# Reordering the head of a fused linear-attention and SwiGLU kernel: three passes over the contraction, a second issuing queue, a shorter warm-up

## The chip, the cores and the metric

The kernel runs on one core of a Trainium2 chip. Its time is the device time of one execution in microseconds (us), the median of several runs. A core has TensorE (matrix products, called PE in the profile), VectorE (DVE), ScalarE (ACT), GpSimd (POOL) and SyncE (SP), which here only issues DMA transfers. The engines run at the same time and wait for each other on semaphores. ScalarE can issue transfers too, from its own queue.

## What is computed

For x of 2048 tokens by 640 the reference mixes two branches by a gate per token, all in bf16:

```python
g = sigmoid((x * gate_w).sum(-1, keepdims=True))
return g * A(x) + (1 - g) * B(x)
# A: q, k, v = x @ wqkv in 32 heads of 20; phi(y) = concat(softmax(y @ w_phi), softmax(-y @ w_phi)) per head
#    kv = phi_k^T v;  z = sum of phi_k;  o = phi_q kv / (phi_q z + 1e-6);  A = o @ wo
# B: (silu(x @ w_gate) * (x @ w_up)) @ w_down, with 1728 hidden columns
```

## The kernel before, in words

**Tiling.** The contraction over the 640 columns of x is cut into five chunks of 128 (index c), the tokens into four blocks of 512 (bt) for branch B and 16 tiles of 128 for branch A. The hidden columns of branch B come in 14 groups of 128 (index k; the last has 64). x is loaded already transposed by DMA into `xT` (chunk, token). The gate weights lie in `wg`, the up weights in `wu`, both (chunk, column).

**Branch B.** For a block and a group, five matmuls of 128x128 by 512 columns give the gate product in one PSUM bank, five more the up product in another. `ffn_tail` takes them on: tanh on ACT, a scalar-tensor-tensor step on DVE (which frees the gate's bank), a copy on ACT (which frees the up's), and a product on POOL into `hT`. `down` multiplies `hT` by `wd`.

**Branch A.** `premult` folds w_phi into the q and k weights; `ktile` and `qtile` make the softmax features (`features`), DVE doing most of that work; the q features and the result `ob` are transposed by DMA on SP (`eT`, `oT`) before TensorE uses them.

**What sets the order.** Nothing is left to a scheduler on the chip. `_build` collects tasks, each with an engine, an assumed cost, what it depends on, a priority, and buffers it takes and gives. `_Plan.run` plays them through on the host, always starting on a free engine the ready task of lowest priority number, and the order it finds is the program's order on each engine. The waits on semaphores that the chip needs are put in from the real data accesses. A `load` has an assumed landing time (`land`), to which `L_SLACK` is added where it is over 13 us; loads of one engine are chained, so they go out in the order written. `E_SLACK` and `O_SLACK` are added to the assumed ends of the eT and oT transposes. `K_AT`, `K_EACH`, `Q_AT`, `Q_EACH`, `PRE_AT` are times in the plan before which a tile's features, or a folding of weights, aren't started. All these numbers change only the order, never what is computed.

**The head.** The first thing TensorE can do is groups 0 to 3 (`HD = 4`) of the first token block: 4 groups x 2 products x 5 chunks = 40 matmuls in all eight PSUM banks. Before it, `warm` runs dummy matmuls on a constant. `load_head` loads pieces of the first 512 gate or up columns, `load_x` pieces of x, and `ffn_head` orders the 40 matmuls by the pieces: gate then up on chunks 0-1, then gate of groups 0-1 on chunks 2-3 and chunk 4, gate of groups 2-3 on chunks 2-4, up on chunks 2-4. All the loads are issued by SP; the first eight are the head's. ACT begins with its table load (for tanh and exp), done for the small task called `table`; later it issues one tiny transfer, the gate column `gw`, held until 11.0 in the plan.

Of the kernel before, what the change touches and what calls it, by code (L numbers as in the profile page):

```python
# [6 lines left out]
P = 128  # L7
S_TOK = 2048
D = 640
H = 32  # L10
DH = 20
F_FFN = 1728
# [224 lines left out]
class _Plan:  # L237
# [98 lines left out]
def _mm(*cols):  # L336
    return sum(c / 2400.0 + 0.003 for c in cols)


def _build(  # L340
# [13 lines left out]
    pe, act, dve, pool, sp = nc.tensor, nc.scalar, nc.vector, nc.gpsimd, nc.sync  # L354
    run = tr.run
# [54 lines left out]
    ps = nc.alloc_psum_tensor("ps", [P, 8 * 512], F32)  # L410
# [11 lines left out]
    def one(b, c0, c1, r0=0, r1=P):  # L422
        return ps[r0:r1, b * 512 + c0:b * 512 + c1]
# [56 lines left out]
    v1ones = places(v1all)[:, :, :, DH]  # L480
    v1pad = v1all.rearrange("p (g x) -> p g x", x=WIN)[:, :, WIN - 1]

    L_SLACK, E_SLACK, O_SLACK = 1.0, 1.4, 1.0
    chain = {}

    def load(eng, dst, src, land, prio, transpose=False, name="load", cost=0.06):

        t = add(eng, cost, lambda: dma(eng, dst, src, transpose=transpose), prio=prio, lat=2.0, name=name)
        t.land = land
        t.slack = L_SLACK if land > 13 else 0.0  # L490
        t.after = chain.get(eng)
        chain[eng] = t
        return t

    def rows(a):
        return a.rearrange("(c p) j -> p c j", p=P)
# [50 lines left out]
    ph_l = load("sp", wph[:, :, :], rows(A_w_phi.rearrange("h e f -> (h e) f")), 16.5, -36.2)  # L547
    load_gu(2, "sp", (17.6, 18.8), -36)
    wkT_l = load_wT(1, 21.6, -34)
    load_gu(3, "sp", (23.2, 24.8), -33)  # L550
    wv_l = load("sp", wvg[:, :, 0:D], rows(A_wqkv[:, 2 * D:3 * D]), 27.3, -32)
    xs[2] = load_x(2, -31, (0, 5, 31.0))
    load_gu(4, "sp", (32.4, 33.9), -30)
    wgl[NPC] = load("sp", wg[:, :, 1664:1728], gsrc[:, :, 1664:1728], 34.2, -29)
    wul[NPC] = load("sp", wg[:, :, 1728:1792], usrc[:, :, 1664:1728], 34.6, -28)
    xs[3] = load_x(3, -27, (0, 5, 37.4))
    wqT_l = load_wT(0, 41.5, -26)
    wd_l = [load("sp", wd[:, 0:13, :], rows(B_w_down[0:13 * P, :]), 48.5, -25),
            load("sp", wd[0:64, 13, :], B_w_down[13 * P:F_FFN, :], 49.0, -24)]
    wo_l = load("sp", wo[:, :, :], rows(A_wo), 51.0, -23)  # L560
    xl = [x_[4] for x_ in xs]


# [36 lines left out]

    ones_row = nc.const_aps.tensor(1.0, (P, 512), BF16)

    def warm(banks, before):
        ctx = {}

        def fn():
            for b in banks:
                last = pe.matmul(one(b, 0, 512), lhsT=ones_row[:, 0:P], rhs=ones_row[:, 0:512], start=True, stop=True, skip_group_check=True)
            return last
        b0, b1 = min(banks), max(banks) + 1  # L610
        t = add("pe", 0.427 * len(banks), lambda: run("pe", fn, reads=[], writes=[ps[:, b0 * 512:b1 * 512]]), prio=-10,
                acq=[("bank", ctx, i) for i in range(b0, b1)], rel=[("bank", ctx, i) for i in range(b0, b1)], name="warm")
# [64 lines left out]
    def ffn_head():  # L677
        tsl = slice(0, 512)
        cs = [{} for _ in range(HD)]
        before = warm_t  # L680
        last = {}

        def group(key, c0, c1, parts):
            nonlocal before
            w = wg if key == "g" else wu

            def fn(ks, cc):
                mms([(one(cs[k][key], 0, 512), w[:, c, P * k:P * k + P], xT[:, c, tsl], c == 0, c == 4) for c in cc for k in ks])
            for ks in parts:
                t = add("pe", _mm(*[512] * (len(ks) * (c1 - c0))), lambda ks=ks: fn(ks, range(c0, c1)),  # L690
                        deps=[xs[0][c1 - 1], hw[key, min(c0, 2), ks[-1]]], prio=-5,
                        acq=[("bank", cs[k], key) for k in ks] if c0 == 0 else (), name="head")
# [408 lines left out]
```

## Time and profile before

| | |
|---|---|
| median of 3 runs | 287.67 us (287.45 to 287.74) |
| span of the profiled execution | 285.6 us |
| TensorE busy | 282.2 us (99%), 2050 matmuls |
| DVE, POOL, ACT busy | 223.9, 171.2, 146.2 us |
| weight loads of TensorE (beside its matmuls) | 151.0 us |
| first real matmul | 5.17 us |
| end of the 40 head matmuls | 13.80 us |
| HBM read, written | 8.30 MB, 2.62 MB |

The span runs from the first to the last instruction; the median is 2.0 us above the span of the profiled execution, for which the profile has no row. Matmuls are pipelined: the profile prints 379 ns for one of 512 columns, but in a stream they start 0.216 us apart. "L442" is a line of the kernel; all real matmuls have that line, all dummy ones L608, all DMA issues L470, all ACT operations L452, since helpers record them. SPq and ACTq are the issuing queues: the time beside them is that of issuing, not of the transfer, and "to landing" counts from the start of the issue.

### The profile page before, as it was taken

What the parts mean: (1) busy time and instruction counts of PE and PEld (TensorE: products, weight loads), DVE (VectorE), ACT (ScalarE), POOL (GpSimd) and SP (SyncE); (2) the same over time, 40 slices, a digit from 0 to 9 for tenths busy, and PEclk for the clock granted to TensorE, in tenths of its full rate; (3) what the DMA queues carried; (4) which work ended last, traced back from release to release, by engine and by line L of the source; (5) the groups of instructions that cost most, each with busy time, mean ns of one, the idle gap of its engine ahead of it and who ended that gap; (6) DMA issues with size and microseconds to landing.
All of it is one profiled execution on the core that took longest, in us unless ns stands there. A gap on an engine that the chain in (4) does not pass through costs nothing.

```text
span 285.6 us, 5119 instructions
## 1 busy us (share of the span) xinstructions
PE 282.2 (99%) x2050; PEld 151.0 (53%) x2050; DVE 223.9 (78%) x318; ACT 146.2 (51%) x222; POOL 171.2 (60%) x164
## 2 busy tenths in 40 slices
PE   8999999999999999999999999999999999999996
PEld 3445555455555555655445555555455565545654
DVE  1324299999999999999999977989999978970312
ACT  2555656775756584344563454456655545564110
POOL 5199407686388748663684577676986666665100
DMA  7999999200000000000217517363435335323211
GB/s 178 258 234 268 225 187 330 88 1 1 2 0 2 0 0 2 2 0 0 45 20 82 127 50 143 75 95 76 93 79 96 67 66 117 60 39 75 69 48 46
DMA packets 65848, 23.91 MB, mean 84 GB/s; under 512 B 53984, under 2 KB 65824, under 8 KB 65824
## 3 DMA queue, kind: packets, MB, share of 16 engines
q1 hardware_dynamic: 65168, 23.58, 38.5%
q8 instruction: 16, 0.26, 0.4%
q10 hardware_dynamic: 656, 0.00, 0.1%
q14 instruction: 8, 0.07, 0.1%
HBM read 8.30 MB, written 2.62 MB: 38 GB/s over the span
## 4 chain that ended last, share of the span: by engine, by line
PE 97%; DMA 1%; SPq 0%; DVE 0%; issue 0%
PE ps L442 97%; DMA xT<-in_A_x_dram 1%; SPq L470 0%; DVE xsb L738 0%
## 5 line engine op out<-in xcount | busy, mean ns | idle before, releaser
L905 POOL TENSOR_TENSOR phi<-phi,rc 128x1320 bf16<-128x1320 bf16 x32 | 77.6, 2426 | 37.8 <-DVE rc L899 37.7
L654 POOL TENSOR_TENSOR hT<-hT,us 128x512 bf16<-128x512 bf16 (+1 forms) x56 | 64.1, 1154 | 41.8 <-DVE hT L648 21.2
L442 PE MATMUL ps<-xT,wg 128*128 128x512 bf16 x280 | 69.1, 379 | 0.2 <-DMA xT<-in_A_x_dram 0.2
L442 PE MATMUL ps<-xT,wu 128*128 128x512 bf16 x260 | 64.3, 379 | 0.0
L442 PE MATMUL ps<-wd,hT 128*128 128x512 bf16 (+1 forms) x448 | 63.0, 299 | 0.0
L648 DVE SCALAR_TENSOR_TENSOR hT<-hT,ps 128x512 bf16<-128x512 bf16 (+1 forms) x56 | 37.5, 674 | 20.4 <-ACT hT L452 20.4
L895 DVE TENSOR_REDUCE sm<-phi 128x66 f32<-128x1320 bf16 x32 | 48.5, 1517 | 6.2 <-ACT phi L452 6.0
L452 ACT ACTIVATE phi<-phi 128x1320 bf16<-128x1320 bf16 x32 | 41.6, 1301 | 17.9 <-DVE phi L884 17.6
L452 ACT ACTIVATE hT<-ps 128x512 bf16<-128x512 f32 (+1 forms) x56 | 33.1, 594 | 34.1 <-PE ps L442 33.6
L442 PEld LDWEIGHTS ps<-wd,hT 128*128 128x128 bf16 x448 | 35.0, 98 | 26.9
L442 PE MATMUL ps<-wqk,xT 128*128 128x512 bf16 (+1 forms) x320 | 48.5, 299 | 0.0
L452 ACT ACTIVATE us<-ps 128x512 bf16<-128x512 f32 (+1 forms) x56 | 33.2, 597 | 17.2 <-PE ps L442 15.7
L442 PEld LDWEIGHTS ps<-xT,wu 128*128 128x128 bf16 x260 | 25.3, 98 | 30.9 <-issue 0.3
L442 PEld LDWEIGHTS ps<-xT,wg 128*128 128x128 bf16 x280 | 25.7, 98 | 25.9 <-issue 0.8
L442 PEld LDWEIGHTS ps<-wqk,xT 128*128 128x128 bf16 x320 | 26.2, 98 | 21.2 <-ACT hT L452 0.2
L872 DVE TENSOR_REDUCE mx<-ps 128x33 f32<-128x660 f32 x32 | 26.8, 837 | 9.3 <-PE ps L442 9.2
L452 ACT ACTIVATE xsb<-ps,gs 128x640 bf16<-128x640 f32 x16 | 12.7, 795 | 32.3 <-PE ps L442 32.3
L884 DVE TENSOR_TENSOR phi<-mn,ps 128x660 bf16<-128x660 f32 x32 | 26.3, 821 | 0.4
L880 DVE TENSOR_TENSOR phi<-ps,mx 128x660 bf16<-128x660 f32 x32 | 26.3, 821 | 0.0
L876 DVE TENSOR_REDUCE mn<-ps 128x33 f32<-128x660 f32 x32 | 26.2, 819 | 0.0
L752 POOL TENSOR_TENSOR xsb<-xsb,xb 128x640 bf16<-128x640 bf16 x12 | 16.7, 1395 | 14.3 <-ACT xb L452 14.3
L442 PE MATMUL ps<-wo,oT 128*128 128x512 bf16 (+1 forms) x160 | 24.3, 299 | 0.0
(44 smaller groups left out, 187.9 us busy)
## 6 DMA issues: line engine op xcount, KB each, us to landing
out_dram<-xsb SPq DMA_DIRECT2D x15, 160.0 KB, 2.0
wd<-in_B_w_down_dram SPq DMA_DIRECT2D x1, 2080.0 KB, 9.4
wg<-in_B_w_gate_dram SPq DMA_DIRECT2D x2, 400.0 KB, 4.1
wu<-in_B_w_up_dram SPq DMA_DIRECT2D x2, 400.0 KB, 4.9
wvg<-in_A_wqkv_dram SPq DMA_DIRECT2D x1, 800.0 KB, 6.9
wo<-in_A_wo_dram SPq DMA_DIRECT2D x1, 800.0 KB, 10.7
wg<-in_B_w_gate_dram SPq DMA_DIRECT2D x2, 320.0 KB, 4.2
wu<-in_B_w_up_dram SPq DMA_DIRECT2D x2, 320.0 KB, 4.8
```

The source lines that it names most:

```text
L442: last = pe.matmul(o, lhsT=l, rhs=r, start=st, stop=sp_, skip_group_check=True)
L452: run("act", lambda: act.activation(o, i, func, scale=scale), reads=reads, writes=[o])
L648: dveop(lambda: dve.scalar_tensor_tensor(out=hap, in0=hap, scalar=1.0, in1=g_, op0=ALU.add, op1=ALU.mult), [hap, g_], [hap])
L654: poolop(lambda: pool.tensor_tensor(hap, hap, u_, ALU.mult), [hap, u_], [hap])
L752: poolop(lambda: pool.tensor_tensor(x_, x_, b_, ALU.add), [x_, b_], [x_])
L872: dveop(lambda: dve.tensor_reduce(a, b, AX.X, ALU.max), [b], [a])
L876: dveop(lambda: dve.tensor_reduce(a, b, AX.X, ALU.min), [b], [a])
L880: dveop(lambda: dve.tensor_tensor(o_, a, b, ALU.subtract), [a, mx[:, ctx["st"], :]], [o_])
L884: dveop(lambda: dve.tensor_tensor(o_, a, b, ALU.subtract), [b, mn[:, ctx["st"], :]], [o_])
L895: dveop(lambda: dve.tensor_reduce(a, b, AX.X, ALU.add), [b], [a])
L905: poolop(lambda: pool.tensor_tensor(a, a, b, ALU.mult), [a, r], [a])
```

## The change

The head's 40 matmuls are cut anew into three passes over the contraction, chunk 0, chunks 1-2 and chunks 3-4, each pass for gate and then up of all four groups (in the last pass, gate by pairs of groups and up group by group). The loads are cut the same way: x in three transfers, gate and up in three pieces each. SP now begins with the three x transfers. The gate piece of chunk 0 is the first load of ACT's queue (priority -43, ahead of the table task at -20); the up piece of chunk 0 and both pieces of chunks 1-2 follow it there (-15 to -13, behind the table task). The pieces of chunks 3-4 stay on SP, behind x. The warm-up has 4 + 4 dummy matmuls of 384 columns instead of 4 + 6 of 512. The assumed landing times of all loads, two slacks and the plan's start times are set anew; the plan's assumed cost of the first group of four matmuls is multiplied by 1.6.

```diff
-    L_SLACK, E_SLACK, O_SLACK = 1.0, 1.4, 1.0
+    L_SLACK, E_SLACK, O_SLACK = 1.0, 1.8, 1.6
...
-    def load_head(key, c0, c1, k0, k1, land, prio):
+    HEAD_C = (0, 1, 3, 5)
+
+    def load_head(eng, key, i, land, prio):
         w, src = (wg, gsrc) if key == "g" else (wu, usrc)
-        t = load("sp", w[:, c0:c1, k0 * P:k1 * P], src[:, c0:c1, k0 * P:k1 * P], land, prio)
-        for k in range(k0, k1):
-            hw[key, c0, k] = t
-        return t
-    load_head("g", 0, 2, 0, HD, 3.9, -43)
-    xa = load_x(0, -42, (0, 2, 5.25))
-    load_head("u", 0, 2, 0, HD, 6.9, -41)
-    load_head("g", 2, 5, 0, 2, 7.4, -40.5)
-    xs[0] = xa + load_x(0, -40, (2, 4, 8.8), (4, 5, 9.3))
-    wgl[0] = load_head("g", 2, 5, 2, HD, 10.0, -39.5)
-    wul[0] = load_head("u", 2, 5, 0, HD, 11.3, -39)
-    load_gu(1, "sp", (12.5, 13.7), -37)
-    xs[1] = load_x(1, -36.5, (0, 5, 16.4))
+        c0, c1 = HEAD_C[i], HEAD_C[i + 1]
+        hw[key, i] = load(eng, w[:, c0:c1, 0:HD * P], src[:, c0:c1, 0:HD * P], land, prio, cost=0.5 if eng == "act" else 0.06)
+        return hw[key, i]
+    load_head("act", "g", 0, 3.4, -43)
+    xs[0] = load_x(0, -42, (0, 1, 3.45), (1, 3, 4.9), (3, 5, 7.1))
+    load_head("act", "u", 0, 4.5, -15)
+    load_head("act", "g", 1, 5.5, -14)
+    load_head("act", "u", 1, 6.4, -13)
+    wgl[0] = load_head("sp", "g", 2, 8.0, -39.5)
+    wul[0] = load_head("sp", "u", 2, 8.5, -39)
+    load_gu(1, "sp", (9.5, 10.5), -37)
+    xs[1] = load_x(1, -36.5, (0, 5, 15.0))
...
+    WARM_N = 384
+
...
-                last = pe.matmul(one(b, 0, 512), lhsT=ones_row[:, 0:P], rhs=ones_row[:, 0:512], start=True, stop=True, skip_group_check=True)
+                last = pe.matmul(one(b, 0, WARM_N), lhsT=ones_row[:, 0:P], rhs=ones_row[:, 0:WARM_N], start=True, stop=True, skip_group_check=True)
...
-    warm_t = warm((4, 5, 6, 7, 4, 5), warm((0, 1, 2, 3), None))
+    warm_t = warm((4, 5, 6, 7), warm((0, 1, 2, 3), None))
...
-        group("g", 0, 2, [(0, 1, 2, 3)])
-        group("u", 0, 2, [(0, 1, 2, 3)])
-        group("g", 2, 4, [(0, 1)])
-        group("g", 4, 5, [(0, 1)])
-        group("g", 2, 5, [(2, 3)])
-        group("u", 2, 5, [(0,), (1,), (2,), (3,)])
+        for i in range(2):
+            for key in "gu":
+                group(key, HEAD_C[i], HEAD_C[i + 1], [(0, 1, 2, 3)])
+        group("g", 3, 5, [(0, 1), (2, 3)])
+        group("u", 3, 5, [(0,), (1,), (2,), (3,)])
...
-    K_AT, K_EACH, Q_AT, Q_EACH = 30.0, 6.08, 120.8, 8.05
-    PRE_Q = 10.06
+    K_AT, K_EACH, Q_AT, Q_EACH = 28.00, 6.108, 120.54, 7.973
+    PRE_Q = 10.07
     PRE_EACH = 2.2
-    PRE_AT = 23.6
+    PRE_AT = 22.6
```

The later loads keep their order on SP; their assumed landing times are about 1.2 us earlier.

More of the change, by code (lines that the diff above doesn't have):

```diff
@@ L542, in _build @@
-    xs[0] = xa + load_x(0, -40, (2, 4, 8.8), (4, 5, 9.3))
-    wgl[0] = load_head("g", 2, 5, 2, HD, 10.0, -39.5)
-    wul[0] = load_head("u", 2, 5, 0, HD, 11.3, -39)
-    load_gu(1, "sp", (12.5, 13.7), -37)
-    xs[1] = load_x(1, -36.5, (0, 5, 16.4))
[L547 to L560, printed above, removed]
+        c0, c1 = HEAD_C[i], HEAD_C[i + 1]
@@ new lines, in _build @@
+    xs[1] = load_x(1, -36.5, (0, 5, 15.0))
+    ph_l = load("sp", wph[:, :, :], rows(A_w_phi.rearrange("h e f -> (h e) f")), 15.2, -36.2)
+    load_gu(2, "sp", (16.4, 17.6), -36)
+    wkT_l = load_wT(1, 20.4, -34)
+    load_gu(3, "sp", (22.0, 23.6), -33)
+    wv_l = load("sp", wvg[:, :, 0:D], rows(A_wqkv[:, 2 * D:3 * D]), 26.1, -32)
+    xs[2] = load_x(2, -31, (0, 5, 29.8))
+    load_gu(4, "sp", (31.2, 32.7), -30)
+    wgl[NPC] = load("sp", wg[:, :, 1664:1728], gsrc[:, :, 1664:1728], 33.0, -29)
@@ L561, in _build @@
+    wul[NPC] = load("sp", wg[:, :, 1728:1792], usrc[:, :, 1664:1728], 33.4, -28)
+    xs[3] = load_x(3, -27, (0, 5, 36.2))
+    wqT_l = load_wT(0, 40.3, -26)
+    wd_l = [load("sp", wd[:, 0:13, :], rows(B_w_down[0:13 * P, :]), 47.3, -25),
+            load("sp", wd[0:64, 13, :], B_w_down[13 * P:F_FFN, :], 47.8, -24)]
+    wo_l = load("sp", wo[:, :, :], rows(A_wo), 49.8, -23)
     xl = [x_[4] for x_ in xs]
@@ L607, in fn @@
             for b in banks:
[L608 removed]
+                last = pe.matmul(one(b, 0, WARM_N), lhsT=ones_row[:, 0:P], rhs=ones_row[:, 0:WARM_N], start=True, stop=True, skip_group_check=True)
             return last
         b0, b1 = min(banks), max(banks) + 1
[L611 removed]
+        t = add("pe", 0.32 * len(banks), lambda: run("pe", fn, reads=[], writes=[ps[:, b0 * 512:b1 * 512]]), prio=-10,
                 acq=[("bank", ctx, i) for i in range(b0, b1)], rel=[("bank", ctx, i) for i in range(b0, b1)], name="warm")
@@ L688, in fn @@
                 mms([(one(cs[k][key], 0, 512), w[:, c, P * k:P * k + P], xT[:, c, tsl], c == 0, c == 4) for c in cc for k in ks])
+            i = HEAD_C.index(c0)
             for ks in parts:
-                t = add("pe", _mm(*[512] * (len(ks) * (c1 - c0))), lambda ks=ks: fn(ks, range(c0, c1)),
-                        deps=[xs[0][c1 - 1], hw[key, min(c0, 2), ks[-1]]], prio=-5,
+                t = add("pe", _mm(*[512] * (len(ks) * (c1 - c0))) * (1.0 if c0 or key == "u" else 1.6), lambda ks=ks: fn(ks, range(c0, c1)),
+                        deps=[xs[0][c1 - 1], hw[key, i]], prio=-5,
                         acq=[("bank", cs[k], key) for k in ks] if c0 == 0 else (), name="head")
```

## The prediction

> **What bounds the kernel now.** I read the page's first part, then the chain that ended last in order of time, then who waited for whom on TensorE, and last the timeline of the first 14 us for each queue.
>
> ```profile
> PE 282.2 (99%) x2050; PEld 151.0 (53%) x2050; DVE 223.9 (78%) x318; ACT 146.2 (51%) x222; POOL 171.2 (60%) x164
> ```
>
> The chain (start, length, what):
>
> ```profile
> 1.32 3.72 DMA xT<-in_A_x_dram
> 5.04 0.14 issue
> 5.17 278.13 PE ps L442 x2040
> ```
>
> TensorE's waits (total, times, longest):
>
> ```profile
> PE ps L608 <- PEq L1085: 0.8, 1, 0.8
> PE ps L442 <- DMA xT<-in_A_x_dram: 0.2, 1, 0.2
> ```
>
> From 5.17 to 283.3 us TensorE does 2040 real matmuls without one recorded wait. Ahead of them stands only the first x transfer, with ten dummy matmuls beside it. So the end moves with two things: when the stream of real matmuls starts, and what new holes or slow matmuls the change puts into it. DVE, ACT and POOL are off this chain.
>
> Timeline of the start, by queue and engine (start, length):
>
> ```profile
> 0.80 0.45 SPq L470 DMA_DIRECT2D wg<-in_B_w_gate_dram  x1
> 1.32 1.32 SPq L470 DMA_TRANSPOSE xT<-in_A_x_dram  x1
> 3.82 1.23 SPq L470 DMA_TRANSPOSE xT<-in_A_x_dram  x1
> ...
> 5.09 1.26 SPq L470 DMA_TRANSPOSE xT<-in_A_x_dram  x1
> ...
> 0.80 1.28 ACT L452 ACT_TABLE_LOAD   x1 [0.80 <-PEq L1085]
> 10.12 0.60 ACT L452 ACTIVATE hT<-ps 128x512 bf16<-128x512 f32 x1 [7.82 <-PE ps L442]
> 10.13 0.41 ACTq L470 DMA_DIRECT2D wvg<-in_gate_w_dram  x1
> 10.61 0.59 ACT L452 ACTIVATE hT<-ps 128x512 bf16<-128x512 f32 x1
> ```
>
> Two chunks of x cost SP 1.23 and 1.32 us to issue, one chunk (at 5.09) 1.26: the price is per transfer, not per chunk. And ACT's queue issued the gate column at 10.13 although the second tanh, which is ahead of it in the program, started at 10.61: the queue runs ahead of the engine.
>
> TensorE (start, length of the group):
>
> ```profile
> 4.21 0.72 PE L608 MATMUL ps<-const-bfloat16-1.0 128*128 128x512 bf16 x2
> 5.17 1.89 PE L442 MATMUL ps<-xT,wg 128*128 128x512 bf16 x8 [0.24 <-DMA xT<-in_A_x_dram]
> ...
> 13.80 1.24 PE L442 MATMUL ps<-xT,wg 128*128 128x512 bf16 x5
> ```
>
> The warm-up's weight loads stand 0.43 us apart up to 4.21, 512 columns at half rate. From 5.17 on 40 head matmuls take 8.63 us to 13.80, 0.2157 each, full rate. The last two warm-up matmuls take 0.72 in all, where half rate would give about 1.06 (the pair at 3.36): the rate doubled inside them, near 4.45, some 3.6 us after the first matmul. (The granted clock is printed as 1.00 throughout, so only the spacing shows this.)
>
> Times from issue to landing, in the DMA view of narrow windows (the first gate piece, the first x), and the least of all x transfers in the view of xT's tile:
>
> ```profile
> wg<-in_B_w_gate_dram SPq DMA_DIRECT2D x1, 256.0 KB, 2.9
> xT<-in_A_x_dram SPq DMA_TRANSPOSE x1, 3.7
> ...
> DMA to landing us min/median/max: 3.1/5.3/9.8
> ```
>
> The 3.1 is the single chunk's; the second two-chunk transfer took 3.9, the later pieces of weights 3.3 to 3.8.
>
> **The change, part by part.** The sum is for the moment the head's 40 matmuls end: 13.80 in the profiled execution. That execution has a span of 285.6 us; the median of the runs is 287.67, 2.0 more, and I carry the difference over unchanged.
>
> *First x chunk and first gate piece.* Both queues start at 0.80, SP with one chunk of x, ACT with a gate piece of 128 KB. The single chunk of before landed 3.1 us after its issue, the first two-chunk one 3.7, and the output transposes of the late phase, alone on the queue, 2.6. So x chunk 0 lands at 3.4 to 4.5; I take 3.75, nearer the one-chunk row, since nothing is ahead of it. A 256 KB weight piece, first on SP, took 2.9; ACT's half piece beside x lands by about 3.7. With 0.13 us from landing to matmul (5.04 to 5.17) the head starts at 3.9, against 5.17.
>
> *Shorter warm-up.* Eight matmuls of 384 columns at half rate: 8 x 0.427 x 384/512 = 2.56 us, from 0.84 to 3.4. It no longer covers the wait for x (a hole of 0.5 us to 3.9), and the first real matmuls run at half rate until about 4.45: 0.55/0.427 = 1.3 matmuls, then 2.7 x 0.2157 = 0.58. The first four end at 5.04; half rate has cost 0.28 us.
>
> *Up piece of chunk 0* (needed at 5.04). ACT issues it behind the table load. If the queue runs past the load, as it ran past the tanh, it goes out near 1.3 and lands by 4.2 (2.9 later). If it is held until the load's end near 2.6, it lands at 5.5. I take the first, the nearer row.
>
> *Chunks 1-2* (needed at 5.90, after four more matmuls). SP issues x at 0.80 + 1.26 + 0.06 = 2.12. The two two-chunk transfers of before took 3.7 and 3.9, the one-chunk one 3.1; a crowded start (1.15 MB asked for at once, 248 GB/s in 5 to 10 us) could make it 4.4. So it lands at 5.2 to 6.5; I take 3.8 later, 5.92, and the matmul at 6.05: a wait of 0.15 us. The gate and up pieces of chunks 1-2, 256 KB each, from ACT near 1.8 and 2.3, at 3.4 later: 5.2 and 5.7, before their use at 6.05 and 7.8.
>
> *Chunks 3-4.* SP issues x at 3.4, weights at 4.7 and 5.3; with 3.9 and 3.8 they land at 7.3, 8.5 and 9.1, used at 9.5 and 11.2. Covered. From 6.05 the other 32 matmuls need 32 x 0.2157 = 6.90: the head ends at 12.95 instead of 13.80, **0.85 us earlier**. With the outer values: 12.6 (start 3.5, no later wait) to 13.55 (x at 6.5).
>
> *Later loads.* SP's queue reaches the next gate piece near 5.8 instead of 7.55 and the next x near 6.9 instead of 8.65, so all that follows goes 1.2 to 1.7 us earlier, more than TensorE does. Before, the two next weight pieces landed at 12.05 and 13.3 for use at 13.80 and 14.88: covered either way. ACT's added issues (four, about 0.45 each) lie before 4 us; its first tanh is at 10.12.
>
> *PSUM.* The first pair of gate results now ends with matmul 28, near 12.95 - 12 x 0.2157 = 10.4, as against 10.1; tanh (0.60) and the DVE step (0.69) free a bank by 11.7, before 12.95. Nothing.
>
> *New due times, slacks, hold times.* They only reorder TensorE's stream. TensorE waited nowhere for an eT or oT; the larger slacks put their users later still. I put 0; it can't gain, as nothing is lost there now. If one user comes too early, the nearest rows are the transposes' 3.6 and 2.6 us to landing, of which a part would be waited: 1 to 2 us.
>
> Sum: 287.67 - 0.85 = **286.8 us**. What follows the last matmul (one DVE step, the last stores) is untouched.
>
> **Rivals.**
>
> *A, as above, 0.60:* 286.4 to 287.1.
>
> *B, ACT's pieces come late, 0.20:* the table load stands ahead of the first piece, or holds the others back. With the load first, the piece goes out at 2.1 and lands 2.9 later, at 5.0: the head starts at 5.13, ends near 13.75, 287.6, the change doing nothing. With only the others held, the gate piece of chunks 1-2 goes out near 3.15, lands at 6.55, and the head ends at 6.7 + 6.90 = 13.6: 287.5. For it: the load took 1.28 us as ACT's first instruction. Against: the gate column that overtook a tanh.
>
> *C, the rate doubles later, 0.07; the other side:* the place is the half-rate stretch, now under real matmuls. If it lasts to T with a start at 3.9, the head ends at T + (40 - (T - 3.9)/0.427) x 0.2157; that is 13.80 for T = 6.5, so from there the change loses. If it takes the 3.6 us once more, T = 8.05, it is 14.6: **288.5**. For it: the new hole of 0.5 us ahead of the doubling. Against: the before's three times lie within 0.29 us, and a doubling after 5.17 would have cost them half of its lateness. [...]
>
> *D, ACT's queue is served only after SP's transposes, 0.07:* the gate column, 1.2 KB, issued at 10.13, landed 6.1 us later; while SP's next x transposes ran, ACT's queue (q10) moved nothing. The queue table from 10.55 to 14.55, then from 14.5 to 15.5:
>
> ```profile
> q1 hardware_dynamic: 3295, 1.10, 119.5%
> ...
> q1 hardware_dynamic: 855, 0.12, 75.4%
> q10 hardware_dynamic: 656, 0.00, 36.9%
> ```
>
> SP's issue of that x ended at 13.45 and ACT's packets came about 1.1 us later. If the head's three x transfers (issued to 4.65) do the same to ACT, its first piece moves from 5.8 and lands near 6.8: the head ends at 6.9 + 8.6 = 15.5, 289.4. Against: that was one transfer of five chunks, issued ahead of the column; here the first piece goes out with the first x and the next two before the second. [...]
>
> *E, the new order puts a hole further on, 0.06:* 1 to 2 us by the price above, 288 to 289.
>
> **How the numbers follow.** Changes under 0.2% (0.58 us) can't be told from none here: faster is below 287.1, slower above 288.25. A lies below (0.60); B is the same (0.20), with some of C and E (0.03); the rest of C, D and E is slower (0.17). The predicted time is A's, 286.8; its own range 286.4 to 287.1. The range from 286.3 (A's best with the runs' spread) takes in B and stops short of C, D and the dearer half of E, at 288.0: about 0.17 left out above, little below.
>
> **What would show it.** Right: the first head matmul between 3.5 and 4.4, one or two matmuls at 0.43 spacing, the gate pass of chunks 1-2 starting near 6.05, the stream after the head beginning near 12.95, TensorE's waits on DMA 0.5 to 0.8 us in all within the first 7 us, and no other wait. Wrong: ACT's first issue behind its table load, or its second after 2.5 (B); 0.43 spacing beyond 6.5 (C); q10's packets only after 5 us (D); a wait of TensorE for eT, oT, DVE or POOL (E). A faster start with the same end would mean that the gain was given back further on.

## The result and the profile after

The changed kernel took **291.35 us** (median of 6 runs, 288.85 to 291.41) against 287.71 for the kernel before, run beside it (287.45 to 288.02). The ratio is 1.0102, with a 95% interval of 1.0081 to 1.0123: it is slower by 3.6 us, where 0.9 us of gain was forecast. The profiled execution took 291.38, with a span of 289.7 us against 285.6 before.

From the page of the changed kernel, TensorE's share of the span and the granted clock in 40 slices:

```profile
PE 280.7 (97%) x2011; PEld 151.2 (52%) x2048; DVE 224.5 (77%) x318; ACT 145.9 (50%) x222; POOL 170.9 (59%) x164
...
PEclk9799999999999999999999999999999999999999
```

(37 matmul records are missing from this trace; the weight loads are all there.) The clock row is new: in its second slice, from 7.2 to 14.5 us, the granted clock was 0.7. The timeline of TensorE at the start (start, length, what, and the idle time before with what ended it) shows the whole loss:

```profile
0.84 2.72 PE L611 MATMUL ps<-const-bfloat16-1.0 128*128 128x384 bf16 x8 [0.84 <-PEq L1088]
4.57 1.02 PE L442 MATMUL ps<-xT,wg 128*128 128x512 bf16 x4 [1.01 <-DMA xT<-in_A_x_dram]
5.43 1.03 PE L442 MATMUL ps<-xT,wu 128*128 128x512 bf16 x4
9.35 2.35 PE L442 MATMUL ps<-xT,wg 128*128 128x512 bf16 x8 [2.89 <-DMA xT<-in_A_x_dram]
11.49 3.16 PE L442 MATMUL ps<-xT,wu 128*128 128x512 bf16 x8
14.49 1.89 PE L442 MATMUL ps<-xT,wg 128*128 128x512 bf16 x8
...
17.94 0.38 PE L442 MATMUL ps<-xT,wg 128*128 128x512 bf16 x1
```

The head starts at 4.57, 0.60 earlier than before. Its pass over chunk 0 runs at full rate (four matmuls start 0.86 apart). Then there is a hole of 2.89 us, and the pass over chunks 1-2 takes 2.14 + 3.00 us from start to start for 16 matmuls, where full rate gives 3.45. The head ends at 17.94 instead of 13.80: 4.1 us, the whole difference of the spans. From there to the last matmul it is 269.22 us, against 269.28 before; nothing is lost or won later.

What TensorE waited for (total, times, longest):

```profile
PE ps L442 <- DMA xT<-in_A_x_dram: 3.9, 2, 2.9
```

And the chain ahead of the end of that hole (start, length, what):

```profile
0.80 1.23 SPq L470
2.03 0.05 issue
2.08 7.13 DMA xT<-in_A_x_dram
9.22 0.14 issue
```

SP issued chunks 1-2 of x on time, at 2.08. They took 7.13 us to land, where the nearest rows of before were 3.7 and 3.9.

The slow matmuls are in the table by stretches of 1 us (each engine's busy time and operations, then the granted clock, the share of the DMA engines and GB/s):

```profile
9.00:10.00 1.00, 0.65 (x4) 0.32 (x5) 0.00 (x0) 0.00 (x0) 0.00 (x0) 1.00 1.18 335
10.00:11.00 1.00, 1.00 (x5) 0.43 (x4) 0.00 (x0) 0.00 (x0) 0.00 (x0) 0.82 1.10 339
11.00:12.00 1.00, 1.00 (x4) 0.39 (x3) 0.00 (x0) 0.00 (x0) 0.00 (x0) 0.50 1.21 304
...
13.00:14.00 1.00, 1.00 (x3) 0.30 (x2) 0.00 (x0) 0.00 (x0) 0.00 (x0) 0.50 1.27 282
14.00:15.00 1.00, 1.00 (x6) 0.48 (x5) 0.00 (x0) 0.00 (x0) 0.00 (x0) 0.97 1.28 291
```

A clock of 0.82 in one stretch is half rate for 0.36 us of it, 0.97 for 0.06: half rate lasted from 10.64 to 14.06, 3.42 us, and cost half of that, 1.71. So the head's delay adds up: -0.60 (start) + 2.89 (hole) + 1.71 (clock) = 4.00 of the 4.14 measured. (The rest is how the hole is counted: the profile lets the last matmul ahead of it end after 0.38 us, where in a stream the next one starts after 0.216.)

Last, what ScalarE did (start, length; ACTq is its issuing queue):

```profile
0.81 0.39 ACTq L470 DMA_DIRECT2D wg<-in_B_w_gate_dram  x1
1.24 1.28 ACT L452 ACT_TABLE_LOAD   x1 [1.24 <-PEq L1088]
1.31 0.39 ACTq L470 DMA_DIRECT2D wu<-in_B_w_up_dram  x1
1.72 0.46 ACTq L470 DMA_DIRECT2D wg<-in_B_w_gate_dram  x1
2.21 0.61 ACTq L470 DMA_DIRECT2D wu<-in_B_w_up_dram  x1
```

All four of its pieces went out by 2.21, three of them during the table load. ACT's queue was neither late nor starved. What it carried is the suspect: by 2.82 it had 768 KB under way beside x. The DMA view of the stretch from 4 to 9 us shows what that did to the 16 DMA engines. After:

```profile
DMA packets 2142, 0.85 MB, mean 169 GB/s; under 512 B 1733, under 2 KB 2142, under 8 KB 2142
...
q1 hardware_dynamic: 1701, 0.43, 69.8%
q10 hardware_dynamic: 441, 0.42, 43.4%
```

Before, with everything on SP's queue (q1):

```profile
DMA packets 2952, 1.13 MB, mean 227 GB/s; under 512 B 1922, under 2 KB 2952, under 8 KB 2952
...
q1 hardware_dynamic: 2952, 1.13, 99.2%
```

With ACT's queue (q10) beside SP's, the same engines moved a quarter less in this stretch, 169 instead of 227 GB/s (from 1 to 9 us 168 instead of 199). A packet of q10 held its engine 0.434 x 16 x 5 us / 441 = 79 ns on average, one of the kernel before 0.992 x 80 us / 2952 = 27 ns, but these differ in size: 0.42 MB / 441 is 0.95 KB, 1.13 MB / 2952 is 0.38 KB. Like with like, by the sizes in the trace's packets, one of 1024 bytes took 84 ns on average instead of 62, and one of 256 bytes (the transposes) 33 instead of 20. (In the version with one queue, below, they took 66 and 35, so slow transposes are not a mark of the second queue alone.)

The two queues did not move evenly either. SP's issue of chunks 1-2 had ended at 3.37. From 3.5 to 4.25 us the changed kernel shows

```profile
q10 hardware_dynamic: 160, 0.16, 93.6%
q1 hardware_dynamic: 21, 0.00, 1.6%
```

160 packets of ACT's queue and 21 of SP's. In the run below in which ACT holds its pieces back, SP's queue moved 473 packets in the same stretch.

### The profile page after: what moved, and what is told of

Read it like the earlier page. It is cut to its first block, busy times and chain, and to the rows that moved or that the text cites. A ratio compares the mean times of both kernels' runs of the same rounds, so it can differ in the third digit from the quotient of the medians.

```text
span 289.7 us, 5086 instructions
## 1 busy us (share of the span) xinstructions
PE 280.7 (97%) x2011; PEld 151.2 (52%) x2048; DVE 224.5 (77%) x318; ACT 145.9 (50%) x222; POOL 170.9 (59%) x164
## 4 chain that ended last, share of the span: by engine, by line
PE 76%; DVE 20%; DMA 2%; issue 1%; SPq 0%
PE ps L442 76%; DVE sm L898 5%; DVE mx L875 3%; DVE phi L887 3%; DVE mn L879 3%; DVE phi L883 3%; DMA xT<-in_A_x_dram 2%; DVE hT L651 2%; DVE rc L902 1%; SPq L470 0%; DVE kvacc L949 0%; DVE kvacc L951 0%; DVE xsb L741 0%
## 5 line engine op out<-in xcount | busy, mean ns | idle before, releaser
L442 PE MATMUL ps<-xT,wg 128*128 128x512 bf16 x271 | 68.1, 381 | 4.3 <-DMA xT<-in_A_x_dram 3.9
L442 PE MATMUL ps<-xT,wu 128*128 128x512 bf16 x256 | 65.0, 385 | 0.1
L442 PE MATMUL ps<-wqk,xT 128*128 128x128 bf16 (+1 forms) x314 | 47.7, 297 | 0.3
L442 PE MATMUL ps<-wo,oT 128*128 128x128 bf16 (+1 forms) x151 | 22.6, 294 | 0.6
```

Of the source, the lines that this page charges most:

```text
L442: last = pe.matmul(o, lhsT=l, rhs=r, start=st, stop=sp_, skip_group_check=True)
```

## The experiments

The expectations name the prediction's rivals by their letters A to E. Beside them stand **M** (ACT's copies and SP's transposes of x, in flight together, slow each other, and this is the hole) and **W** (the shorter warm-up alone costs time, through the hole ahead of the head and the clock). "Head end" is the start of the first matmul after the 40 of the head.

### The same loads on one queue

All nine head loads of the changed kernel go out from SP, in the order of their use; ACT issues none (empty ACT tasks in the plan keep TensorE's order as it was).

```diff
-    load_head("act", "g", 0, 3.4, -43)
-    xs[0] = load_x(0, -42, (0, 1, 3.45), (1, 3, 4.9), (3, 5, 7.1))
-    load_head("act", "u", 0, 4.5, -15)
-    load_head("act", "g", 1, 5.5, -14)
-    load_head("act", "u", 1, 6.4, -13)
+    load_head("sp", "g", 0, 3.4, -43)
+    xs[0] = load_x(0, -42, (0, 1, 3.45))
+    load_head("sp", "u", 0, 5.1, -41.8)
+    xs[0] += load_x(0, -41.7, (1, 3, 4.9))
+    load_head("sp", "g", 1, 5.6, -41.5)
+    load_head("sp", "u", 1, 6.4, -41.4)
+    xs[0] += load_x(0, -41.3, (3, 5, 7.1))
```

> The changed kernel with the four weight pieces taken off ScalarE's queue: SyncE issues all nine head loads, in the order gate 0, x 0, up 0, x 1-2, gate 1-2, up 1-2, x 3-4, gate 3-4, up 3-4. The order of TensorE's work is unchanged. Theory M (weights from a second queue in flight beside x's transposes slow the transposes): x 1-2 lands 3.5 to 4.0 us after its issue instead of 7.1, so near 7.0 to 7.5; the hole in TensorE before the pass of chunks 1-2 is under 1 us; the clock stays full after the warm-up; the head ends at 14.0 to 14.5 and the time is 287.7 to 288.4. Rival S (x's transposes, cut in three, are slow by themselves, or the start just asks for too many bytes): x 1-2 still takes about 7 us from its issue and lands near 10, the time is 291 or more.

289.37 us against 287.74, ratio 1.0054 (1.0038 to 1.0070). Chunks 1-2 of x now land 3.83 us after their issue. But the head ended at 16.32, not at the 14.0 to 14.5 that I expected, and the time lies above the expected 287.7 to 288.4, though below the rival's 291. Its timeline:

```profile
4.33 1.86 PE L442 MATMUL ps<-xT,wg 128*128 128x512 bf16 x4 [0.77 <-DMA xT<-in_A_x_dram]
5.99 1.91 PE L442 MATMUL ps<-xT,wu 128*128 128x512 bf16 x4
9.40 1.90 PE L442 MATMUL ps<-xT,wg 128*128 128x512 bf16 x8 [1.50 <-DMA wg<-in_B_w_gate_dram]
```

and its chain:

```profile
4.44 4.92 DMA wg<-in_B_w_gate_dram
```

The gate piece of chunks 1-2, last in a row of five issues, took 4.92 us and is the next thing that is late; and the first eight matmuls ran at half rate (0.43 each) up to 8.15. M holds for x of chunks 1-2, but one queue is no cure here: six finely cut transfers ahead of the second pass took too long by themselves here, and x of chunks 3-4, issued behind four weight pieces on the same queue, took 5.56 us.

### x with the field to itself

ACT holds its last three pieces back until all three x transfers of the head have landed.

```diff
+        def fn():
+            if name == "late":
+                tr._emit_waits(eng, dict([x_ev[2]]))
+            dma(eng, dst, src, transpose=transpose)
-        t = add(eng, cost, lambda: dma(eng, dst, src, transpose=transpose), prio=prio, lat=2.0, name=name)
+        t = add(eng, cost, fn, prio=prio, lat=2.0, name=name)
```

> The changed kernel, but ScalarE's last three head pieces (up 0, gate 1-2, up 1-2) wait until all of x for the head has landed, so that x 1-2 and x 3-4 move with nothing beside them. Theory M: x 1-2 lands 3.1 to 3.9 us after its issue (5.2 to 6.0) and x 3-4 near 7.5. Rival S: x 1-2 still lands after 8. The time itself is worse than the changed kernel's under both, since the weights come late: 292 to 294.

x landed as the prediction had it: chunk 0 at 3.60 (3.75 forecast, 4.44 in the changed kernel), chunks 1-2 at 6.17, 4.07 us after their issue, chunks 3-4 3.82 after theirs. That is the second confirmation of M, in the changed kernel's own order of issue. From the DMA view of windows that hold one issue of chunks 1-2 (KB, median us to landing), first the changed kernel's line, then this one's:

```profile
xT<-in_A_x_dram SPq DMA_TRANSPOSE x1, 7.1
```

```profile
xT<-in_A_x_dram SPq DMA_TRANSPOSE x1, 4.1
```

Then ACT's three pieces flew beside the next x, five chunks, and all of them crawled:

```profile
wg<-in_B_w_gate_dram ACTq DMA_DIRECT2D x1, 256.0 KB, 9.4
wu<-in_B_w_up_dram ACTq DMA_DIRECT2D x1, 256.0 KB, 10.4
wu<-in_B_w_up_dram ACTq DMA_DIRECT2D x1, 128.0 KB, 5.9
xT<-in_A_x_dram SPq DMA_TRANSPOSE x1, 12.5
```

In the kernel before, pieces of 256 to 384 KB took 2.9 to 5.2 us, and this x, issued at 8.65, took 7.8. So the slowing goes both ways, and it moved with the overlap when the overlap was moved. The time, 300.21 us in one run, is far above the expected 292 to 294: TensorE waited 7.6 us for an up piece and 2.0 for a gate piece, and the granted clock was 0.50 from 9.08 to 22.72, 13.6 us.

### A longer warm-up in the changed kernel

Sixteen more dummy matmuls, of 512 columns, so that TensorE is busy until x and the pieces are there. (`warm` takes their number of columns and their cost in the plan as two more arguments.)

```diff
-    warm_t = warm((4, 5, 6, 7), warm((0, 1, 2, 3), None))
+    warm_t = warm((4, 5, 6, 7) * 4, warm((4, 5, 6, 7), warm((0, 1, 2, 3), None)), 512, 0.0)
```

> The changed kernel with sixteen more dummy matmuls of 512 columns between the warm-up and the head, so that the head starts near 7.5 and its pass of chunks 1-2 follows chunk 0 without a hole. Loads unchanged. Theory C (the hole of 2.9 us put TensorE's clock back to half for one window of 3.4 us, which cost 1.7 us of the 3.6): x 1-2 still lands at 9.2, no half-rate stretch after the warm-up, head ends near 16.3, time 289.5 to 289.9 in every run instead of 291.4 in most and 289 in some. Rival (the half rate has another cause, or all of the loss is the late x): 291.4 as before.

289.68 us (289.44 to 290.6, one of the four runs above the expected 289.9), ratio 1.0071 (1.0049 to 1.0094): 1.67 us faster than the changed kernel, although the first real matmul starts 3.2 us later.

```profile
0.84 7.06 PE L611 MATMUL ps<-const-bfloat16-1.0 128*128 128x384 bf16 x24 [0.84 <-PEq L1088]
7.74 1.02 PE L442 MATMUL ps<-xT,wg 128*128 128x512 bf16 x4
...
9.47 1.89 PE L442 MATMUL ps<-xT,wg 128*128 128x512 bf16 x8
...
16.37 1.24 PE L442 MATMUL ps<-xT,wg 128*128 128x512 bf16 x5
```

x still came late (chunks 1-2 took 6.59 us), but no hole is left for TensorE and no slow stretch: the head ends at 16.37, 1.57 earlier. The granted clock was 1.00 from 9 to 12 us. So the half-rate stretch is a price of the hole and worth what the table by stretches above says, 1.7 us. The 1.9 us that are left over the kernel before are the late loads and the late start that covers them.

### The shorter warm-up alone

The kernel before with eight dummy matmuls of 384 columns instead of ten of 512.

```diff
-                last = pe.matmul(one(b, 0, 512), lhsT=ones_row[:, 0:P], rhs=ones_row[:, 0:512], start=True, stop=True, skip_group_check=True)
+                last = pe.matmul(one(b, 0, 384), lhsT=ones_row[:, 0:P], rhs=ones_row[:, 0:384], start=True, stop=True, skip_group_check=True)
-    warm_t = warm((4, 5, 6, 7, 4, 5), warm((0, 1, 2, 3), None))
+    warm_t = warm((4, 5, 6, 7), warm((0, 1, 2, 3), None))
```

> The kernel before with only its warm-up shortened, to eight dummy matmuls of 384 columns; loads and order unchanged. It opens a hole of 1.7 us (3.4 to 5.17) ahead of the head. [...] Rival (the short warm-up is enough, as my prediction had it: the rate doubles near 4.5 whatever stands in the hole): 287.7, no change.

289.27 us (287.6 to 290.01) against 287.62, ratio 1.0044 (1.0025 to 1.0062). x came as before (5.00), and still:

```profile
5.13 3.57 PE L442 MATMUL ps<-xT,wg 128*128 128x512 bf16 x8 [1.57 <-DMA xT<-in_A_x_dram]
8.49 2.22 PE L442 MATMUL ps<-xT,wu 128*128 128x512 bf16 x8
...
15.73 1.24 PE L442 MATMUL ps<-xT,wg 128*128 128x512 bf16 x5
```

Eight matmuls start over 3.36 us, 0.42 each: half rate up to 9.16, not to the 4.45 of before. W holds: dummy matmuls that ended 1.57 us ahead of the data cost about 1.65 us, with nothing else changed. The eight runs spread from 287.6 to 290.0, far wider than before's, and two of them (287.6 and 287.7) show no loss, so the price depends on something that varies from run to run.

### The plan's numbers alone

The kernel before with the two slacks, the plan's start times and the landing times of the loads behind the second x as in the changed kernel.

```diff
-    L_SLACK, E_SLACK, O_SLACK = 1.0, 1.4, 1.0
+    L_SLACK, E_SLACK, O_SLACK = 1.0, 1.8, 1.6
...
-    wv_l = load("sp", wvg[:, :, 0:D], rows(A_wqkv[:, 2 * D:3 * D]), 27.3, -32)
+    wv_l = load("sp", wvg[:, :, 0:D], rows(A_wqkv[:, 2 * D:3 * D]), 26.1, -32)
...
-    K_AT, K_EACH, Q_AT, Q_EACH = 30.0, 6.08, 120.8, 8.05
+    K_AT, K_EACH, Q_AT, Q_EACH = 28.00, 6.108, 120.54, 7.973
```

> The kernel before with only the plan's numbers of the changed kernel: the two slacks, the start times of features and foldings, the landing times of the loads behind the second x. Head, loads and warm-up unchanged. My theory is that the changed kernel loses everything in its head and nothing later: 287.5 to 288.1, no wait of TensorE beyond those of before. Rival E (the new order opens holes further on): 288.5 or more, with waits of TensorE for DVE, POOL or a transpose after 20 us.

290.3 us (289.56 to 290.48), ratio 1.0084 (1.0069 to 1.0098); I had expected hardly any change. In its profile TensorE waits on one load:

```profile
PE ps L442 <- DMA wvg<-in_A_wqkv_dram: 1.4, 1, 1.4
```

The v weights landed at 29.29, and the order wanted them at 27.94; in the kernel before they landed at 28.13 and were first used at 30.17. So most of the wait, 1.16 us, is a later landing, of which no run shows the cause; but the earlier use left no room for it. The stream behind the head is 2.1 us longer than before, of which this wait is 1.4; where the rest lies is open. This is rival E's mechanism, but not a part of the changed kernel's loss. There these weights are first used at 34.31, 16.37 us after the head's end, as in the kernel before (30.17, 16.37 after 13.80); here they were wanted 14.06 after the head's end (13.88). The new numbers fit the new head and are wrong with the old one. Which of them moved the use, the landing times (1.2 us earlier), the slacks or the start times (`K_AT` is 2.0 earlier), was not separated. What the run shows is how sharp the plan is: numbers that are off by one or two us put a wait of 1.4 us into a stream that had none.

### Fewer bytes on ACT's queue

The changed kernel with only the two 128 KB pieces of chunk 0 from ACT; the pieces of chunks 1-2 go out from SP, behind x of chunks 1-2.

```diff
     load_head("act", "g", 0, 3.4, -43)
-    xs[0] = load_x(0, -42, (0, 1, 3.45), (1, 3, 4.9), (3, 5, 7.1))
     load_head("act", "u", 0, 4.5, -15)
-    load_head("act", "g", 1, 5.5, -14)
-    load_head("act", "u", 1, 6.4, -13)
+    xs[0] = load_x(0, -42, (0, 1, 3.45), (1, 3, 4.9))
+    load_head("sp", "g", 1, 5.6, -41.5)
+    load_head("sp", "u", 1, 6.4, -41.4)
+    xs[0] += load_x(0, -41.3, (3, 5, 7.1))
```

> The changed kernel with half of the move to ScalarE undone: gate and up of chunk 0 (128 KB each) stay on ScalarE's queue, gate and up of chunks 1-2 (256 KB each) go to SyncE behind x 1-2. Order of TensorE's work unchanged. Theory M, by dose: the two small pieces are through by about 4.2, when x 1-2 begins to move, so x 1-2 lands 3.8 to 4.3 us after its issue at 2.1 (5.9 to 6.4) instead of 7.1; the gate piece of chunks 1-2 then binds and lands at 8 to 9, the hole is 1.5 to 2.5 us, the time 289 to 290.5, in two groups 1.7 us apart. If x 1-2 still lands after 8, the large pieces were not what slowed it.

288.95 us (287.48 to 289.48), ratio 1.0030 (1.0013 to 1.0048): 2.4 us faster than the changed kernel. Chunks 1-2 of x land 3.87 us after their issue, so 256 KB beside x does not cost them what 768 KB does. Their gate piece landed at 7.43, earlier than expected, and no hole opened ahead of it; the time is just below the expected 289 to 290.5, and the runs form no two clear groups. Chunk 0 came later than in the changed kernel, at 5.07 instead of 4.44 (why is open), and behind the short warm-up that left

```profile
5.20 1.86 PE L442 MATMUL ps<-xT,wg 128*128 128x512 bf16 x4 [1.64 <-DMA xT<-in_A_x_dram]
6.86 1.91 PE L442 MATMUL ps<-xT,wu 128*128 128x512 bf16 x4
```

with half rate (0.42 to 0.43 each) until 9.15 and a head end of 15.76.

### Both taken back: small pieces and the old warm-up

The kernel above with the ten dummy matmuls of 512 columns of before.

```diff
-    warm_t = warm((4, 5, 6, 7), warm((0, 1, 2, 3), None))
+    warm_t = warm((4, 5, 6, 7, 4, 5), warm((0, 1, 2, 3), None))
```

(with 512 columns again in the matmul and the plan's cost for no more than four of them per call, so that the order stays.)

> The changed kernel with only the two 128 KB pieces of chunk 0 on ScalarE's queue (as in the run before it of that kind) and with the warm-up of the kernel before, ten matmuls of 512 columns, in place of eight of 384. If what kept that run at 288.95 was the short warm-up (a hole ahead of the head, the clock at half rate up to 9.15), the chunks 1-2 of x land near 6.0 and their gate piece near 7.5 as there, the granted clock is full by 7.2, the head ends at 14.2 to 14.6, and the time is 288.0 to 288.4. If the order of the loads keeps it, the head ends at 15.5 or later and the time stays at 288.9.

287.84 us (287.34 to 288.19, 10 runs) against 287.65, ratio 1.0003 (0.9994 to 1.0012): the loss is gone, within 0.12%.

```profile
0.84 4.27 PE L619 MATMUL ps<-const-bfloat16-1.0 128*128 128x512 bf16 x10 [0.84 <-PEq L1096]
4.95 1.03 PE L442 MATMUL ps<-xT,wg 128*128 128x512 bf16 x4
...
7.41 1.90 PE L442 MATMUL ps<-xT,wg 128*128 128x512 bf16 x8 [0.56 <-DMA wg<-in_B_w_gate_dram]
...
14.32 1.24 PE L442 MATMUL ps<-xT,wg 128*128 128x512 bf16 x5
```

Full rate almost from the start, a wait of 0.56 us on the gate piece of chunks 1-2, head end 14.32, in the expected 14.2 to 14.6; the time came out better than the expected 288.0 to 288.4. The stream behind the head is 269.22 us with all the new plan numbers in it, so these cost nothing where the head fits them. The changed kernel and the three versions around it make a table (medians, us; in the second row 24 dummy matmuls on the left, ten on the right):

| | four pieces from ACT (768 KB) | two pieces (256 KB) |
|---|---|---|
| warm-up ends ahead of the data | 291.35 (as changed) | 288.95 |
| warm-up reaches the data | 289.68 | 287.84 |

Either step alone gives part back (1.67 and 2.40), both together 3.51 of the 3.64.

### Three smaller questions on the kernel before

*Two weight pieces from ACT.* The up piece of chunks 0-1 and the first gate piece of chunks 2-4, 448 KB, issued by ACT instead of SP.

```diff
-    load_head("u", 0, 2, 0, HD, 6.9, -41)
-    load_head("g", 2, 5, 0, 2, 7.4, -40.5)
+    load_head("u", 0, 2, 0, HD, 6.9, -15, "act")
+    load_head("g", 2, 5, 0, 2, 7.4, -14, "act")
```

> The kernel before with two of its weight pieces (up of chunks 0-1, 256 KB, and gate of chunks 2-4 for groups 0-1, 192 KB) moved to ScalarE's queue behind the table load; pieces, passes, warm-up and order of TensorE's work unchanged. SyncE issues x 2-3 and x 4 some 1.2 us earlier than before. Theory M: the copies on the second queue run beside x and slow it; x 0-1, 5.04 before, lands at 5.5 to 6.5, x 2-3 not before 8 in spite of its earlier issue; a hole opens in the head and the time is 288.3 to 290. Rival (a second queue only saves issue time): x 0-1 at 5.0, x 2-3 near 6.5, no wait, 287.7 or a little less.

290.25 us (288.59 to 290.36), ratio 1.0067 (1.0044 to 1.0089). ACT's issues went out at 0.81 and 1.33, ahead of its table load (1.87) and not behind it, and the first x, issued at 1.33 (1.32 before), took 4.93 us instead of 3.72. From the chain:

```profile
1.33 4.93 DMA xT<-in_A_x_dram
```

M once more for the first x, which landed at 6.26 (5.5 to 6.5 expected), in the old order and with nothing else touched; x 2-3 landed at 7.67, not after 8. But the engines lost little here: 193 GB/s from 1 to 9 us, 199 before. That points to the 448 KB themselves, asked for 1.9 to 2.0 us earlier than from SP's queue and moved beside x, more than to engines that moved less. The runs fell into two groups, near 288.6 and 290.3; the profile is of the lower one, and the median lies just above the expected 288.3 to 290.

*x first.* The first two loads of SP exchanged.

```diff
-    load_head("g", 0, 2, 0, HD, 3.9, -43)
-    xa = load_x(0, -42, (0, 2, 5.25))
+    xa = load_x(0, -43, (0, 2, 5.25))
+    load_head("g", 0, 2, 0, HD, 3.9, -42)
```

> The kernel before with its first two loads exchanged on SyncE: x 0-1, then the gate piece. One queue throughout. x 0-1 then moves alone from its issue at 0.80 and lands near 4.0, the gate piece near 4.7; but the warm-up's ten matmuls end at 4.9 to 5.1, so the head can start only about 0.1 us earlier: 287.4 to 287.7, no measurable change. If x came later instead (after 5), 288 or more.

288.53 us (288.22 to 290.27), ratio 1.0052 (1.0032 to 1.0073), where I expected no change. x landed at 4.00, 1.0 earlier; but the gate piece, behind a transpose on the same queue, took 3.68 us from an issue at 2.19, instead of the 2.9 it took before, where it was first. It landed at 5.86 (4.7 expected), and the head started at 5.91. Six of the ten runs lie at 288.2 to 288.6 and four at 290.1 to 290.3; the profile is of the first group.

*The first gate piece from ACT.* 256 KB issued by ACT at 0.81, ahead of its table load, and one dummy matmul fewer.

```diff
-    load_head("g", 0, 2, 0, HD, 3.9, -43)
+    load_head("g", 0, 2, 0, HD, 3.9, -43, "act")
...
-    warm_t = warm((4, 5, 6, 7, 4, 5), warm((0, 1, 2, 3), None))
+    warm_t = warm((4, 5, 6, 7, 4), warm((0, 1, 2, 3), None))
```

> The kernel before with one thing moved: its first gate piece (chunks 0-1, 256 KB) goes out on ScalarE's queue ahead of the table load, and the warm-up has nine dummy matmuls instead of ten. SyncE thus begins with x 0-1. Order of TensorE's work unchanged. If a second queue is harmless while it moves one piece that is through before x starts: x 0-1 lands near 4.5 instead of 5.04, all of SyncE's loads are 0.5 us earlier, and the time is 287.2 (0.5 us faster). If any piece on the second queue slows x (theory M in its strong form): x 0-1 lands at 5 or later and the time is 287.7 or more.

287.69 us against 287.74, ratio 0.9999 (0.9990 to 1.0008): no change. x 0-1 landed at 4.67, between the two expectations. The head starts at 4.81, 0.36 earlier, and ends at 14.22, later: in this profile the rate doubled only at 6.42.

### Two tries at a faster start

*All of x in one go.* One queue again, with the three x transfers directly behind the first gate piece and the other five weight pieces behind them.

```diff
-    load_head("act", "g", 0, 3.4, -43)
+    load_head("sp", "g", 0, 3.4, -43)
     xs[0] = load_x(0, -42, (0, 1, 3.45), (1, 3, 4.9), (3, 5, 7.1))
-    load_head("act", "u", 0, 4.5, -15)
-    load_head("act", "g", 1, 5.5, -14)
-    load_head("act", "u", 1, 6.4, -13)
+    load_head("sp", "u", 0, 5.1, -41.6)
+    load_head("sp", "g", 1, 5.6, -41.5)
+    load_head("sp", "u", 1, 6.4, -41.4)
```

> The one-queue variant of the changed kernel with another order on SyncE: gate 0, then all three x transfers, then the five weight pieces, so that transposes and copies meet only twice. Theory M2 (what costs is a transpose and a copy in flight at the same time, on one queue too, where they meet at each change from one to the other): the last head piece lands at 10.5 to 11.0 instead of 12.7 in the alternating order, x 1-2 at 6.2 and x 3-4 at 7.4. Rival (alternation on one queue is free, the start is simply bound by bytes): 12.5 or later. The time: up 0 lands near 7.7, the hole before it is 2 us or more and the clock pays for it: 289 to 290.5 either way.

292.39 us, ratio 1.0157 (1.0138 to 1.0176), above the expected 289 to 290.5. A gain from keeping the x transfers together was not borne out: the last head piece landed at 13.19, against 12.70 with x and weights alternating on one queue. The up piece of chunk 0 came at 8.97, TensorE waited 3.68 us for it, and the clock was at half from 6.94 to 13.77, 6.8 us, about twice the stretch of the changed kernel.

*x in two transfers.* The run with the first gate piece from ACT, and chunks 2 to 4 of x as one transfer.

```diff
-    xs[0] = xa + load_x(0, -40, (2, 4, 8.8), (4, 5, 9.3))
+    xs[0] = xa + load_x(0, -40, (2, 5, 8.8))
```

> The kernel before with its first gate piece (256 KB) issued by ScalarE and nine warm-up matmuls, which alone came out at 287.69 against 287.74, and beside that chunks 2 to 4 of x as one transfer in place of two. If the head is then held by the last weight piece behind SyncE's issues (it landed at 10.98), one issue less of about 1.3 us brings that piece to about 9.8, the head ends 0.2 to 0.4 earlier and the time is 287.3 to 287.5. If the start of the head or the clock's doubling sets it, no change: 287.7. If the larger x transfer lands behind its use (it is three chunks, used from about 9.3 on), a wait of up to 0.5 us shows in front of chunk 2 and the time is up to 288.2.

287.95 us against 287.65, ratio 1.0005 (0.9996 to 1.0014): no change. The larger transfer landed behind its use. From its chain:

```profile
3.32 5.65 DMA xT<-in_A_x_dram
```

TensorE waited 0.28 us for it. Nor did SP save an issue: SP's timeline shows the one transfer of three chunks at

```profile
3.32 3.35 SPq L470 DMA_TRANSPOSE xT<-in_A_x_dram  x1
```

3.35 us where the two of before took 2.53. No version here beats the kernel before.

## Why the prediction was wrong

**The step that failed: "I take 3.8 later, 5.92" for x of chunks 1-2, with 6.5 as the worst.** They landed at 9.22, 7.13 us after the issue. I took the duration from rows in which every head load shared one queue, and priced the crowd of the start as 0.6 us at most. What no row of before showed is large copies on ACT's queue beside x transposes on SP's. With that overlap x took 7.13 and 6.59 us; with ACT held back 4.07, with fewer bytes on ACT 3.87 and 3.44, with one queue 3.83. That the copies in flight beside x do it is shown from both sides, by removal here and by adding them to the kernel before (4.93 us instead of 3.72 for its first x). How they do it is shown in part. They took a share of the engines while x waited (from 4 to 9 us a share of 43.4%, beside 69.8% for SP's queue), and the engines moved less. An estimate from the rates of 1 to 9 us: at 199 GB/s instead of 168 the bytes of these 8 us would have been through in 8 x 168 / 199 = 6.75, 1.25 us earlier; that is the lower rate's part of the 3.3 us by which x missed 5.92, and the larger part is the share. My bound for the crowd had 248 GB/s for 1.15 MB, and x came last of these bytes. No run separates the two parts, and why the engines moved less is not shown.

**The same cause in the neighbouring terms.** ACT's gate and up pieces of chunks 1-2 landed at 6.56 and 9.03, not at 5.2 and 5.7. Chunk 0 of x landed at 4.44, at the edge of my 3.4 to 4.5 and not at 3.75; with ACT held back it landed at 3.60, but with only 256 KB from ACT at 5.07 and 4.72, so for chunk 0 the bytes on ACT's queue are not the whole cause. The head's start gained 0.60 and not 1.27.

**"Half rate has cost 0.28 us" for the shorter warm-up.** Wrong in place and size. In the profile the rate had doubled by 4.57, so the start cost nothing; the 2.9 us hole that followed brought 3.42 us of half rate under the second pass, 1.71 us. I had asked only when the rate doubles first, not whether it would fall again, and I let the cover of the wait for x go at the price of half-rate matmuls alone. Alone, in the kernel before, the shorter warm-up cost about 1.65 us.

**"The price is per transfer, not per chunk."** True of one and two chunks (1.23 to 1.32 us each). But the last x of the head took SP 2.86 us to issue (4.19 for the two together), three chunks in one 3.35, and five 4.8 in the kernel before. So the next gate piece went out at 7.46 instead of 5.8, and the next x at 8.97 instead of 6.9, later than before. It cost nothing, as the head itself was late.

**What held.** ACT's queue ran past its table load (issues at 1.31, 1.72 and 2.21, the load from 1.24 to 2.52), and the up piece of chunk 0 landed at 4.19 (4.2 forecast). Chunks 3-4 were covered, but by luck: they landed at 9.99, 10.75 and 11.51, up to 2.7 us later than forecast, and only because the second pass was late itself did TensorE not wait for them (9.5 was the forecast use of the first two). PSUM cost nothing. The new plan numbers cost nothing: 269.22 us behind the head here, and in the version with both steps taken back; but put onto the old head they made the stream 2.1 us longer, so "0" was the right sum and too firm a reason.

**The rivals.** A fell with the x term. B is refuted: the issues went out at 0.81 to 2.21, beside the load (1.24 to 2.52). D had the right two parties and the wrong victim: ACT's packets moved from 1.8 us on, and x paid, 3.3 us later than forecast. ACT's queue did not starve: from 3.5 to 4.25 us it moved 160 packets and SP's moved 21. Whether SP's transposes were ready to move then the trace does not tell, and how the engines choose between the two queues is not shown. Against D I had asked only whether ACT's queue would be held up, and from there went on to the sum of 286.8; I did not ask what its copies would do to x beside them (7.13 us instead of my 3.8), and here the engines also moved less (169 instead of 227 GB/s from 4 to 9 us). C had the right party, the clock, and the wrong event: in this profile the first doubling was not late, and the rate fell again after a wait that I had at 0.15 us and that was 2.89; that cost 1.7 us. The late doubling that C describes came in other versions with the short warm-up: in three of them, half rate lasted until 8.15 to 9.16. The first doubling came 3.6 us after the first matmul in the kernel before, 3.7 us or less after it in the changed kernel (by 4.57), and 8.3 us after it with the short warm-up alone (9.16); what sets that moment is not shown. The granted clock was 0.50 for 3.42 us in the changed kernel (a wait of 2.89 us), for 6.8 in the run with all of x in one go (a wait of 3.68) and for 13.6 in the run with x to itself (waits of 7.6 and 2.0). E did not happen in the changed kernel.

## What to carry to other kernels

In these runs a transfer's landing time held only for what flew beside it: x of chunks 1-2 took 3.44 to 4.07 us with one queue, with small pieces on ACT's queue or with ACT held back, and 7.13 and 6.59 us beside 768 KB on ACT's queue. When a change moves large copies to a second queue, price the transposes of the first queue from a row where the two kinds overlap, or put only small pieces on the second queue (256 KB here: 3.87 and 3.44 us). Dummy matmuls are a cover for a wait, not only for the first clock doubling: with 24 of them the changed kernel took 289.68 us instead of 291.35. If they end ahead of the data, or a hole opens behind them, look for half rate in the matmuls that follow; here a hole of 2.89 us was followed by 3.42 us of it, a loss of 1.71. (Gaps of 0.77, 1.57 and 1.64 us ahead of the head left half rate until 8.15 to 9.16 in three profiles, those of the one queue, of the shorter warm-up alone and of the fewer bytes on ACT's queue; gaps of 0.75 us, with all of x in one go, and of 1.01, in the changed kernel, did not.) This new start order moved the head's start by 0.60 us, and one such hole with its half rate cost 4.60.

## What the runs showed of the hardware

- Copies from ACT's queue and transposes from SP's took longer in flight together: x of chunks 1-2 7.13 us in the changed kernel, 3.83 with one queue and 4.07 with ACT held back; with ACT held back, its 256 KB copies beside the five-chunk x 9.4 and 10.4 us, where pieces of 256 to 384 KB took 2.9 to 5.2 in the kernel before. The engines moved 169 GB/s in the changed kernel and 227 before over 4 to 9 us, 168 and 199 over 1 to 9. Of the two queues of the changed kernel, ACT's moved 160 packets and SP's 21 from 3.5 to 4.25 us.
- In the changed kernel ACT issued three transfers at 1.31, 1.72 and 2.21 during its table load (1.24 to 2.52).
- In the changed kernel a hole of 2.89 us with a granted clock of 1.00 was followed, 1.3 us after its end, by 3.42 us at 0.50. Of its six runs two lie at 288.85 and 289.45, 2.5 and 1.9 below the median and so somewhat more than this stretch costs; whether it was missing in these two was not seen, as only one at 291.38 was profiled.
- The issue of an x transfer on SP had no fixed price: the third of the head, two chunks, took 2.86 us in the changed kernel and 1.23 in the version with one queue.
